# A two-layer transformer kernel on one core: weight loads swapped at the start, larger pieces at the end, and a new written-out order for TensorE

## The chip, the cores and the metric

The kernel runs on one NeuronCore of a Trainium2 chip. The metric is the device time of one execution, in microseconds. Besides the runs there is one profiled execution, from which all traces come. TensorE (PE) does the matmuls, and its weight loads (PEld) overlap them; VectorE (DVE) and ScalarE (ACT) move results out of PSUM and do softmax, LayerNorm and activation arithmetic; GpSimd (POOL) clears a buffer and does one small power; SyncE (SP) issues nearly all DMAs. Every engine works through its instructions in order.

## The reference

Two layers over `x` of 2048 rows by 576 columns (bf16). Each layer is attention with a recurrent memory and then a gated FFN, with the same weights in both layers:

```python
for s in range(n_seg):                       # 64 segments of 32 rows
    h = concat([mem, layernorm(x)[s]])       # 8 memory rows + 32 rows
    q, k, v = h @ Wq, h @ Wk, h @ Wv         # 32 heads of 128
    p = softmax(where(mask, q @ k.T * scale, -1e9))
    o = (p @ v) @ Wo
    mem, out[s] = o[:8], o[8:]               # the next segment reads mem
x = x + out
x = x + (silu(layernorm(x) @ w1) * (layernorm(x) @ w3)) @ w2   # 4608 wide
```

A segment needs the memory of the segment before it, so attention is a chain of 64 steps in each layer.

## The kernel before

**Steps.** The second layer runs eight segments behind the first (`LAG = 8`), so there are 72 steps. In most of them a segment of layer 0 and one of layer 1 are handled together (80 columns instead of 40); the first eight steps have layer 0 alone and the last eight layer 1 alone. After every four steps (128 rows) an FFN "job" follows for each layer that has the rows, cut into 18 pairs of 128-column blocks ("pr"), whose work is spread over the next steps. The last job has one layer only, and nothing to be spread over.

**Letters.** All TensorE work is cut into batches, one letter each. In a step: `Q` and `q` are the Q and K projections of four heads (units u0 to u7; `Q` the four 128-row chunks of the weights, `q` the last 64 rows, which need the last memory piece); `S` scores of eight heads (groups g 0 to 3); `T` transposes of the probabilities; `P` probabilities times V; `O` and `o` the output projection; `X`, `x`, `V`, `v` and `G`, `g` the V projection (VX, VM and, for pairs of steps, VG). For the FFN: `F` and `f` the up projections of a pair of blocks, `W` and `w` the down projection of two pairs (first and second layer). `p`, `n`, `a`, `b` and `m` are transposes around LayerNorm and residual. Between `S` and `T` stands the softmax chain: add of the mask, maximum and subtraction, exponential (ACT), sum and reciprocal, product into `PB`. Each letter writes PSUM banks (eight in all), and an eviction on ACT or DVE frees them.

**Order.** PE's order is written out by hand as a string: `ORDER = FIRST + FOUR * 11 + LAST`. FIRST covers the start to a steady state; FOUR is a pass of four steps (224 letters) and is repeated eleven times; LAST is the rest. A planner (`plan`) lays the nodes out in time with a modelled duration for each; PE follows the string, and for the other engines it takes what can start first, then by a priority. Nodes of kind "AD" go to ACT or DVE, whichever the plan has free sooner. So a change of a modelled duration moves evictions between the two engines, and a change of priorities moves DMAs on SP's queue. The emitted instructions are chained in the plan's order on each engine. The modelled duration of an eviction of 512 columns is `ew(512)`, which is 0.49 us on ACT and 0.60 on DVE.

**Weights.** `W` holds Wq and Wk (nine chunks of 4096 columns), `WV` holds Wv, `WO` holds Wo; they stay in SBUF. `load_qk(half)` loads half the heads (ten DMAs, 4.5 MB), `load_v` all of Wv (six DMAs, 4.5 MB), `load_o(g)` a quarter of Wo. The first three are ordered by their priorities. FFN weights do not fit beside them and are loaded pair by pair for each job into two buffers (`W13`, `W2C`). For the last job alone they are loaded into `W` and `WV`, once the last step has read what it needs there: `tail_load` does it in eight pieces of 512 columns, each with four DMAs into `W` (w1 and w3) and one into `WV` (w2), behind the last step's `Q`, `q` and V letters (`qk_done`, `v_done`) and, from the fifth piece, behind an `O` as well. Pair 16 and 17 of that job are kept from the job before. The first `Q` of u0 and of u4 in step 0 carries twelve extra matmuls of 512 columns on the arriving weights, if it comes ahead of its `q`.

Of the kernel before, what the change touches and what calls it, by code (L numbers as in the profile page):

```python
# [13 lines left out]
P = 128  # L14
R64 = 64
D = 576
# [10 lines left out]
NG = 4  # L27
# [153 lines left out]
def ew(*ns):  # L181
    return (actc(*ns), dve(*ns))


def ewh(*ns):
# [2 lines left out]


FIRST = (  # L190
    "maQqqqQQSQqqqQTQSqqQSQSXxvVPTPTOPOTOoooPOoQQQqqVSqqvQQqqSQQqqSQTXPSxTOPTPOTOPoooOoaQQqqqqQSvQVSqQQqTQSqqQSPTPOOT"
    "ooPTPOOooQQqqqvqSVQQQqSTQqqQPSqQOSoTXPTOPTOPxooOoQQpQqqqqQSVSnvqQFffqFQQTSqqPQOToSfFPWTOPfFTOPFOfoooWQQfqqqQSvVF"
    "qfQFQWSqqQFSfQTQPqqfFOTSoWPFTOPfxXTFPOOoooWQQqqfqQQSfqFSvVfqqQFQWSqTQQPFqffTOSoPWOTFPFTOPfaOoooWQFQqqfQSVvqqfFQQ"
    "SqWQQqqqQSTPSTbOPoXTOPTxxPOOoooXqqQpQQqqSVvnQFFSfqQqfqQQTSqfFPQTOPSofWTOPFOTFPWOoooFQqqffQQqSQQQqqgqGTSWPQQfqqFF"
    "fgSSTGGPFgfTOWPOfgGTOPFOooooWQQfqqqFQvSfqFQQfqSVTFQqfFQPSaTWQPfqqFOSoTWFOPffFTOPWOoooFQqqqfQQSWQqqQQSqqTbQSGgqgQ"
    "PGTGPSggOTGPOTOPoooOoQQppqqVqqvSQQnnQFSfqfqFTQQPFSqqfQTwOPWFSoffTOFPwTOPWOoooFQffqqFQwWSQQFfqqfFTGqqgSQPQFWTQSgf"
    "qqGQwPFTSfggOGGPOTwPOOooooWFfqqQQFQqfqvVSQQWFfqqSQwTFPaSqfqQTQwFWPSffTOPFOOTwPWOooooFqqfqQQWqSQQQSqqqQQbQSqggGTG"
    "PGTSggPGTOPOTwPOOoooo"
)
FOUR = (  # L200
    "QqQpQpQqqqvVSSnnQFffqqFQQTFSffqqQPFTWSPOwTFPOTOPwOooooWQQqqqfQSQQQqqqfFGgfSSTFPFQqfqgGQTWwPFTSfggGFPGOTOPOOooooW"
    "wQQqqqfQFQvfqfVSSwFQWQFqffqFWTQPwTFSffqqQOPWoSwTFPFOTOPwWOoooffFQqqQWQSqqqQaQSbQQTQqqqgGSSgPGTGPOTggGPOTwPOOoooo"
)
LAST = (
    "QQpqqqQpSqqQQnVqvSnQTQQPqqSFTSffOPFOTFPfwTOPFOooooWQQqfqqQFwWSfqfQQFGSgfqqQTFPGwSTWFqfgqQQPWTFSfgfgGFwGPOTOPOOoo"
    "oofFWQwQFqfqqQQWSfqVvSQFTFqqfQPQTwSqqfFOQPWwffSFTFPOOTFPWOoooowQQqqqfQQSvqqqVSQWTQQPqqQOTSSbPwvVoXTOPToxPOOooVpp"
    "qqvQQQqqSQQnnQqqfSFQTFPSfqqQTFfSPOOwTWPFfTOPFOoooowQWfqqQQQFvqqfVSSFQQfqqFTWQfqqSQPwTOPoSXfTFPOWOTxfPFOwoooFQQvq"
    "fqVSqqQQWwFTQqfqfSQQPFwFqfqSQTWOPSfFTFWPOTOPwOooooffQFqqQWQSqqqQwFvSfVQTQPWqqQSOQqwTSbPOTXoPToxPOOooQqqqqQpQQSVv"
    "QnqSQFqfqfFQTQqSPSwTOPFFTffoPOTOPwOoooFQqqfqQQqfvSVFQFQSqfqQTQQqfqSFPSXTwPOTFPOTxooPOOoowQQqqvfSVqqqQQQSqQQTSfFP"
    "FTfqqQOoSPwTfOFPFTOPfooOowQQqqqqQSQQSqfqFQVvSfFTwQQqfqPTSFPFTOPOTOPwOooooffpFnwFfffFFFwffFFwfffFFwFwfffFFFwfffFF"  # L210
    "wFwFffffFFww"
)
ORDER = FIRST + FOUR * 11 + LAST

# [1 line left out]
class Opt:  # L216

    qk, qkt, sc, tr, pv, wo, wog, vm = 0.0079, -0.0342, 0.0268, 0.1447, 0.0406, 0.2653, 0.0725, 0.1407
# [4 lines left out]
def make_nodes(em, nseg, pools, o=Opt, dma_bw=230e3, load_bw=400e3):  # L223
# [4 lines left out]
    def node(*a, **k):  # L228
        n = Node(*a, **k)
        nodes.append(n)  # L230
        return n
# [5 lines left out]
    kb = lambda rows, cols: rows * cols * 2  # L237
# [9 lines left out]
    def load(name, nbytes, prio, fn, deps=()):  # L247
        return node("DMA", nbytes / load_bw, fn, deps=deps, prio=prio, name=name, lat=2.0)

    ld_m0 = node("ACT", 0.1, em.load_m0(), prio=-90, name="m0", lat=2.5)  # L250
    ld_h = [load("ldqk", kb(512 + 2 * R64, 4096), half - 9.0, em.load_qk(half)) for half in (0, 1)]
    ld_v = [load("ldv", kb(512 + 2 * R64, 4096), -7.0, em.load_v())]
    ld_o = [load("ldo", kb(1024, 576), g - 6.0, em.load_o(g)) for g in range(NG)]

    b = banks(1)
    m0t = node("PE", 0.3, em.m0_tr(b[0]), deps=[ld_m0], prio=-5, mode="full", acq=b, name="m0tr")
# [42 lines left out]
    def v_nodes(name, t, k, prio, tail_at, emit, strips, deps, tail_deps, free):  # L299

        modes = ("col", "quad") if strips[0][3] == R64 else ("c32", "oct")
        b = banks()
        m_ = node("PE", 8 * 0.2158, emit(b, False), deps=deps, prio=prio, mode=modes[0], acq=b, name=name)
        n = node("PE", 0.2158, emit(b, True), deps=deps + tail_deps, prio=prio + tail_at, mode=modes[1], acq=b, name=name + "t")
        reads_ht.setdefault(t, []).extend([m_, n])
        for r in (0, 1):
            outs = em.v_parts(strips, r)
            b[r].users = len(outs)
            for p0, width, row, blk in outs:
                e = node("AD", ew(512), em.v_ev(b[r], p0, width, row, blk), deps=[m_, n] + free.get(blk // 2, []), prio=prio + 0.01 * (blk // 2),  # L310
                         rel=[b[r]], name=name + "e")
                vx_ev.setdefault((name, t, blk // 2), []).append(e)
        return [m_, n]
# [15 lines left out]

    def vg_out(t, g, b, deps, row):  # L330

        return [node("AD", ew(512), em.v_ev(b[r], row, R64, row, 2 * g + r), deps=deps, prio=t + o.vm + 0.01 * g + (0.05 if row == 0 else 0.0), rel=[b[r]],
                     name="VGe") for r in (0, 1)]

    def vx_pair(t, prio):
# [8 lines left out]
    def step(t):  # L344
        ls = layers_of(t)
        nl = 2 if both(t) else 1
        c80 = 40 * nl
        e = role(t)
# [12 lines left out]
        wos, wots = [], []  # L361
        for g in range(NG):
            qs, qe = [], []
            for u in (2 * g, 2 * g + 1):
                q = Slot("qkt", users=1)
                b = banks()
                pq = t + o.qk + o.ustep * u
                m_ = node("PE", 32 * mm80, em.qk(t, u, b), deps=hx + hm[:1] + ([ld_h[u // 4]] if t == 0 else []),
                          prio=pq, mode="full", acq=[q] + b, name="QK")
                n = node("PE", 4 * mm80, em.qk_tail(t, u, b), deps=hx + hm + ([ld_h[u // 4]] if t == 0 else []), prio=pq + o.qkt, mode="row",  # L370
                         acq=[q] + b, name="QKt")
                rd += [m_, n]
                me[f"QK{u}"], me[f"QKt{u}"] = m_, n
                for r in (0, 1):
                    qe.append(node("AD", ew(256, 64) if nl == 2 else ew(160), em.qk_ev(t, u, r, q, b[r]), deps=[m_, n], prio=t + o.ustep * u,
                                   rel=[b[r]], name="QKe"))
                qs.append(q)
            s = banks(1)[0]
            sme = Slot("sme")
            pf = t + o.gstep * g  # L380
            sc = node("PE", 8 * 0.0165 * nl, em.scores(t, g, qs, s), deps=qe, prio=pf + o.sc, mode="col", acq=[s, sme], rel=qs, name="SC")
            a = node("DVE", dve(320), em.sm_add(t, g, s, sme), deps=[sc], prio=pf, rel=[s], name="add")
            m_ = node("DVE", dve(320, 320) + 0.13, em.sm_max(t, g, sme), deps=[a], prio=pf, name="maxsub")
            c = node("ACT", 0.105 + 320 * 0.000833, em.sm_exp(t, g, sme), deps=[m_], prio=pf, name="exp")
            pb = Slot("pb")
            d = node("DVE", dve(320) + 0.2, em.sm_sum(t, g, sme), deps=[c], prio=pf, name="sum")
# [7 lines left out]
            if paired(t):  # L394
# [3 lines left out]
            b = banks()  # L398
            ot = Slot("ot")
            pv = node("PE", 8 * mm80, em.pv(t, g, pts, b), deps=pe_ + vx_ev["VM", t, g] + vx_ev["VX", t - e, g],  # L400
                      prio=pf + o.pv, mode="full", acq=b + [ot], rel=[pts], name="PV")
            pvs[t, g] = pv
            if paired(t):
# [3 lines left out]
                      acq=[y] if g == 0 else [], name="WO")  # L407
# [6 lines left out]
            wots.append(wot)  # L414
            me[f"SC{g}"], me[f"TR{g}"], me[f"PV{g}"], me[f"WO{g}"] = sc, tr, pv, wo
        if t == nst - 1:
            last_reads[2].extend(wos)
            last_reads[1].extend(me[f"{k}{u}"] for u in range(8) for k in ("QK", "QKt"))
        nxt = [li for li in ls if t - LAG * li + 1 < nseg]
        ye = []  # L420
# [17 lines left out]
        return node("DVE", dve(576), em.post_add(li, g, xr[g], b[0]), deps=[d], prio=prio, rel=b, name="POSTa")  # L438

    last_up = []  # L440
    last_reads = [], [], []
    kept = {}

    def job(j):
# [6 lines left out]
        s0 = 4 * j + 4 if j < ngrp else 4 * j - 4 + LAG  # L451
# [9 lines left out]
        w2_last = {}  # L461
        tail = None
        if last:
            v_done, qk_done, wo_done = last_reads
            tail = []
            for i in range(8):
                late = wo_done[i - 4:i - 3] if i >= 4 else []
                parts = [(0, 9 * 512, qk_done[2 * i:2 * i + 2] + late), (1, 4 * 576, v_done + late)]
                tail.append([load("tail", kb(128, c), s0 + o.tail_at + 0.01 * i, em.tail_load(i, what), deps=dep) for what, c, dep in parts])

        npp = NPR // 2
        for at, pp in enumerate([npp - 1] + list(range(npp - 1)) if last else range(npp)):
            mids, w2s, htts, lds = [], [], [], []
            stays = last and pp == npp - 1
            for pr_ in (2 * pp, 2 * pp + 1):
                prio = s0 + o.ff + (o.win if s0 + 4 < nst else o.last_win) * (2 * at + pr_ % 2) / NPR
# [7 lines left out]
                else:  # L484
# [6 lines left out]
                b = banks()  # L491
# [3 lines left out]
                          acq=b + [htt], rel=rel13, name="FF")  # L495
# [7 lines left out]
            for (bi, g) in ents:  # L503
                b = banks()
# [54 lines left out]
class Emitter:  # L559
# [126 lines left out]
    def tail_load(self, i, what):  # L686

        def f(n):
            T = self.T
            fa = i * 512  # L690
            t13, t2 = T.W[:, :, fa:fa + 512], T.WV[:, i * 4 * D:(i + 1) * 4 * D].rearrange("p (b d) -> p b d", b=4)
            if what != 1:
                for kind, wd in ((0, self.a.w1), (1, self.a.w3)):
                    self.dma(t13[:, 4 * kind:4 * kind + 4], wd[0:4 * P, fa:fa + 512].rearrange("(c p) f -> p c f", p=P))
                for kind, wd in ((0, self.a.w1), (1, self.a.w3)):
                    self.dma(t13[kind * R64:(kind + 1) * R64, 8], wd[4 * P:D, fa:fa + 512])
            if what != 0:
                self.dma(t2, self.a.w2[fa:fa + 512, :].rearrange("(b p) d -> p b d", p=P))
            for h in range(2):
                self.tail_w[2 * i + h] = (t13[:, :, h * 2 * P:(h + 1) * 2 * P], t2[:, 2 * h:2 * h + 2])  # L700
        return f


# [598 lines left out]
```

## Time and profile before

| | |
|---|---|
| five runs: median, lowest, highest | 2703.98, 2696.57, 2706.35 us |
| profiled execution: own time, span | 2704.19, 2702.4 us |
| mean granted TensorE clock | 0.992 |
| busy: PE, DVE, ACT, POOL | 2630.9, 2090.3, 1367.1, 333.6 us |
| DMA: bytes, mean rate | 321.42 MB, 119 GB/s |
| DMAs on the SP queue | 1616 |

The own time is that of the profiled execution by the clock of the runs; the span is the time between its first and last recorded instruction. Busy time is the sum of an engine's instructions without the time it waits, and a busy PE can still be slower than it might be, since matmul ends are modelled. A line of the timeline gives the start, the time, the engine, the source line, the operation, output and inputs, and in brackets the idle time ahead of it with what ended it. Since one helper emits each engine's instructions, the source line says little, and tile names are what to go by: `QKT` is q and k, `SME` and `STAT` the softmax, `PTS` the transposed probabilities, `OT` the attention output, `HTT` the FFN's middle, `XR` the residual rows.

### The profile page before, as it was taken

How to read it: one execution, taken by the hardware profiler on the slowest of the kernel's cores; microseconds unless marked ns; L12 is line 12 of the kernel's file. 1: busy time of each engine (PE TensorE's matmuls, PEld its weight loads, DVE VectorE, ACT ScalarE, POOL GpSimd, SP SyncE). 2: the span in 40 equal slices, each digit the busy share in tenths (PEclk: the TensorE clock that was granted, in tenths of full speed). 3: DMA queues.
4: the chain of work that ended last, by engine and by line, in shares of the span. 5: the costliest groups of instructions: out<-in, count | busy, mean ns of one | idle time of the engine just before them, and what ended most of it. 6: DMA issues, size and time to landing. Idle time of an engine off the chain costs nothing.

```text
span 2702.4 us, 126553 instructions
## 1 busy us (share of the span) xinstructions
PE 2630.9 (97%) x55714; PEld 2227.8 (82%) x55795; DVE 2090.3 (77%) x5376; ACT 1367.1 (51%) x4025; POOL 333.6 (12%) x400
## 2 busy tenths in 40 slices
PE   5999999999999999999999999999999999999998
PEld 3788888888888888888888888888888888888886
DVE  4787887887778778777877877787787777787876
ACT  2655554544546454554545445464545546454553
POOL 1111110110101011010101101010110101011110
PEclk8999999999999999999999999999999999999999
DMA  9064523234342433434243343424234342434358
GB/s 316 4 182 122 160 83 117 85 110 125 99 130 84 118 88 110 125 100 130 82 119 88 110 125 99 130 83 119 88 110 125 99 130 66 133 89 147 114 169 245
DMA packets 483225, 321.42 MB, mean 119 GB/s; under 512 B 26376, under 2 KB 477328, under 8 KB 482160
## 3 DMA queue, kind: packets, MB, share of 16 engines
q1 hardware_dynamic: 479488, 306.22, 38.4%
q8 instruction: 437, 7.16, 1.1%
q0 software_dynamic: 3024, 6.93, 0.9%
q14 instruction: 116, 0.95, 0.1%
q10 hardware_dynamic: 160, 0.16, 0.0%
HBM read 308.49 MB, written 2.36 MB: 115 GB/s over the span
## 4 chain that ended last, share of the span: by engine, by line
PE 87%; ACT 4%; DMA 4%; DVE 3%; issue 1%; SPq 0%; POOL 0%; DVEq 0%; ACTq 0%; POOLq 0%
PE bank L578 87%; ACT V L581 3%; DMA W<-in_B_w_dram 2%; DVE SME L584 1%; DMA W<-in_A_Wk_dram 1%; DMA WV<-in_A_Wv_dram 1%; DVE STAT L584 1%; DVE V L584 1%; ACT SME L581 0%; ACT XTB L581 0%; SPq L587 0%; ACT QKT L581 0%; ACT PTS L581 0%; DVE HTT L584 0%; DMA XN<-in_A_x_dram 0%
## 5 line engine op out<-in xcount | busy, mean ns | idle before, releaser
L578 PEld LDWEIGHTS <-W 128*128 128x128 bf16 (+1 forms) x29520 | 1238.6, 98 | 148.9 <-issue 44.0
L578 PE MATMUL bank<-HT,W 128*128 128x80 bf16 (+3 forms) x23040 | 810.2, 196 | 23.0 <-DMA W<-in_A_Wq_dram 10.7
L578 PE MATMUL bank<-XTB,W 128*128 128x256 bf16 (+3 forms) x6480 | 662.7, 261 | 7.4 <-DMA W<-in_B_w_dram 4.4
L581 ACT ACTIVATE QKT<-bank 128x256 bf16<-128x256 f32 (+3 forms) x1587 | 366.0, 316 | 369.4 <-PE bank L578 350.2
L981 POOL MEMSET PB<- 128x1024 bf16 x288 | 274.2, 952 | 1818.6 <-PE bank L578 1316.7
L578 PE MATMUL bank<-OT,WO 128*128 128x80 bf16 (+3 forms) x11520 | 406.8, 198 | 0.7 <-DVE OT L584 0.3
L581 ACT ACTIVATE V<-bank 64x512 bf16<-64x512 f32 (+1 forms) x616 | 346.4, 584 | 110.0 <-PE bank L578 104.9
L578 PEld LDWEIGHTS <-WO 128*128 128x128 bf16 (+1 forms) x11520 | 379.5, 102 | 15.6 <-issue 5.2
L578 PE MATMUL bank<-WV,HT 128*32 128x512 bf16 (+5 forms) x3160 | 358.5, 387 | 14.6 <-issue 9.9
L578 PE MATMUL bank<-W2C,HTT 128*128 128x288 bf16 x2240 | 315.3, 286 | 0.0
L584 DVE TENSOR_TENSOR PB<-SME,STAT 40x128 bf16<-40x128 f32 (+4 forms) x912 | 275.3, 336 | 14.9
L584 DVE TENSOR_REDUCE STAT<-SME 104x8 f32<-104x320 f32 (+1 forms) x576 | 273.9, 475 | 14.3 <-ACT SME L581 8.9
L581 ACT ACTIVATE HTT<-bank 128x512 bf16<-128x512 f32 (+1 forms) x324 | 179.6, 555 | 183.3 <-PE bank L578 181.3
L578 PEld LDWEIGHTS <-HT 128*32 128x32 bf16 (+4 forms) x3240 | 137.5, 97 | 159.0 <-issue 41.5
L584 DVE SCALAR_TENSOR_TENSOR XR<-bank,XR 128x288 f32<-128x288 f32 x576 | 246.5, 450 | 15.7 <-PE bank L578 7.8
L578 PEld LDWEIGHTS <-HTT 128*128 128x128 bf16 x2304 | 209.8, 98 | 48.4 <-issue 0.2
L581 ACT ACTIVATE OT<-bank 128x320 bf16<-128x320 f32 (+1 forms) x398 | 149.3, 405 | 166.7 <-PE bank L578 165.6
L584 DVE CAST QKT<-bank 128x192 bf16<-128x192 f32 (+2 forms) x461 | 125.0, 317 | 136.3 <-PE bank L578 135.1
L584 DVE SCALAR_TENSOR_TENSOR HTT<-HTT,bank 128x512 bf16<-128x512 bf16 (+1 forms) x324 | 202.5, 625 | 34.3 <-ACT HTT L581 30.4
L581 ACT ACTIVATE PTS<-bank 128x320 bf16<-128x320 f32 (+1 forms) x385 | 144.4, 402 | 164.3 <-PE bank L578 127.3
L584 DVE TENSOR_TENSOR HTT<-HTT,bank 128x512 bf16<-128x512 bf16 (+1 forms) x324 | 203.7, 629 | 30.6 <-DVE HTT L584 0.5
L581 ACT ACTIVATE SME<-SME 104x320 f32<-104x320 f32 (+1 forms) x288 | 135.5, 470 | 139.1 <-DVE SME L584 136.6
(61 smaller groups left out, 1805.5 us busy)
## 6 DMA issues: line engine op xcount, KB each, us to landing
W<-in_B_w_dram SPq DMA_DIRECT2D x612, 256.0 KB, 3.5
W2C<-in_B_w_dram SPq DMA_DIRECT2D x306, 288.0 KB, 3.2
W<-in_B_w_dram SPq DMA_DIRECT2D x612, 32.0 KB, 3.2
W<-in_B_w_dram SPq DMA_DIRECT2D x16, 512.0 KB, 8.5
WO<-in_A_Wo_dram SPq DMA_DIRECT2D x4, 1152.0 KB, 16.8
XR<-in_A_x_dram POOLq DMA_DIRECT2D x16, 288.0 KB, 2.8
WV<-in_B_w_dram SPq DMA_DIRECT2D x8, 576.0 KB, 7.2
W<-in_A_Wq_dram SPq DMA_DIRECT2D x8, 512.0 KB, 9.0
```

What stands on the lines that cost most here:

```text
L578: self.ch("PE", self.nc.tensor.matmul(out, lhsT=lhsT, rhs=rhs, start=start, stop=stop, skip_group_check=True, **k))
L581: self.ch("ACT", self.nc.scalar.activation(*a, **k))
L584: self.ch("DVE", getattr(self.nc.vector, fn_)(*a, **k))
L981: return lambda n: self.ch("POOL", self.nc.gpsimd.memset(self.T.PB[:, pb.i], 0.0))
```

## The change

The three strings are replaced; each keeps its length and its count of every letter. Three priorities put `load_v` between the two halves of `load_qk`. The eviction of a V block is modelled with 0.55 us on ACT and 0.60 on DVE, and `S` of a single-layer step with 0.23 us rather than 0.13. The last job's weights come in four pieces of 1024 columns, 20 DMAs in place of 40, without the condition on `O`. In the built program 173 instructions move from ACT to DVE over the whole kernel (5366 to 5539 on DVE); in one pass of FOUR, DVE has 20 rather than 14 evictions of QK, 13 rather than 12 of PTS, 11 rather than 10 of OT, 3 rather than 2 of VM and 10 rather than 11 of VG.

```diff
-    "maQqqqQQSQqqqQTQSqqQSQSXxvVPTPTOPOTOoooPOoQQQqqVSqqvQQqqSQQqqSQTXPSxTOPTPOTOPoooOoaQQqqqqQSvQVSqQQqTQSqqQSPTPOOT"
+    "maqQQQQqqqxvXSSVTPTPQqqQQqqSQSOoTOPToPOOooQQQqqqqQSVvSqqQTQQPQqqTSSXPOOToPTOPooxOoQQqqqqQSvQVSqQqQQQqSTqSPTPOOTo"
...
 FOUR = (
-    "QqQpQpQqqqvVSSnnQFffqqFQQTFSffqqQPFTWSPOwTFPOTOPwOooooWQQqqqfQSQQQqqqfFGgfSSTFPFQqfqgGQTWwPFTSfggGFPGOTOPOOooooW"
-    "wQQqqqfQFQvfqfVSSwFQWQFqffqFWTQPwTFSffqqQOPWoSwTFPFOTOPwWOoooffFQqqQWQSqqqQaQSbQQTQqqqgGSSgPGTGPOTggGPOTwPOOoooo"
+    "QqQpQpQqqqVnvSSnQFfqfqFQQTFSqffqQPFTOoSwPWTOPFTOPWOooowQfqqqQQSqqqQQQFSSgffGTFPQFqqfgQGwTWPFSffggGFTGOPOTwPOOooo"
+    "oWQQQqqqqQWSSVvffqFFQTwQPFfqfqFTwWQFSfqfFQPWwSFTOOPWTOPwOooooffFQQqqqWQQSqqqQQSabQqqgQTGgSSPGTggGPGTOPOTwPOOoooo"
 )
...
-    "FTfqqQOoSPwTfOFPFTOPfooOowQQqqqqQSQQSqfqFQVvSfFTwQQqfqPTSFPFTOPOTOPwOooooffpFnwFfffFFFwffFFwfffFFwFwfffFFFwfffFF"
-    "wFwFffffFFww"
...
+    "qqSQPwSTOPfFOTfooPwTFPOOooFfqqQQQvSqqVQwSQTFqqqfQQPSqfFTQPOoSwTFPOFTOPffoOoopwnffffFFFFwFwfffFFFwfffFFFwFwfffFFF"
+    "wffFFwfffFFww"
...
-    ld_h = [load("ldqk", kb(512 + 2 * R64, 4096), half - 9.0, em.load_qk(half)) for half in (0, 1)]
-    ld_v = [load("ldv", kb(512 + 2 * R64, 4096), -7.0, em.load_v())]
-    ld_o = [load("ldo", kb(1024, 576), g - 6.0, em.load_o(g)) for g in range(NG)]
+    ld_h = [load("ldqk", kb(512 + 2 * R64, 4096), 3 * half - 9.0, em.load_qk(half)) for half in (0, 1)]
+    ld_v = [load("ldv", kb(512 + 2 * R64, 4096), -8.0, em.load_v())]
+    ld_o = [load("ldo", kb(1024, 576), g - 5.0, em.load_o(g)) for g in range(NG)]
...
-                e = node("AD", ew(512), em.v_ev(b[r], p0, width, row, blk), deps=[m_, n] + free.get(blk // 2, []), prio=prio + 0.01 * (blk // 2),
+                e = node("AD", (0.55, 0.6), em.v_ev(b[r], p0, width, row, blk), deps=[m_, n] + free.get(blk // 2, []), prio=prio + 0.01 * (blk // 2),
...
-            sc = node("PE", 8 * 0.0165 * nl, em.scores(t, g, qs, s), deps=qe, prio=pf + o.sc, mode="col", acq=[s, sme], rel=qs, name="SC")
+            sc = node("PE", 8 * (0.0165 * nl if nl == 2 else 0.029), em.scores(t, g, qs, s), deps=qe, prio=pf + o.sc, mode="col", acq=[s, sme], rel=qs, name="SC")
...
-            v_done, qk_done, wo_done = last_reads
+            v_done, qk_done = last_reads
             tail = []
-            for i in range(8):
-                late = wo_done[i - 4:i - 3] if i >= 4 else []
-                parts = [(0, 9 * 512, qk_done[2 * i:2 * i + 2] + late), (1, 4 * 576, v_done + late)]
-                tail.append([load("tail", kb(128, c), s0 + o.tail_at + 0.01 * i, em.tail_load(i, what), deps=dep) for what, c, dep in parts])
+            for i in range(4):
+                parts = [(0, 9 * 1024, qk_done[4 * i:4 * i + 4]), (1, 8 * 576, v_done)]
+                tail += [[load("tail", kb(128, c), s0 + o.tail_at + 0.01 * i, em.tail_load(i, what), deps=dep) for what, c, dep in parts]] * 2
...
-            fa = i * 512
-            t13, t2 = T.W[:, :, fa:fa + 512], T.WV[:, i * 4 * D:(i + 1) * 4 * D].rearrange("p (b d) -> p b d", b=4)
+            fa = i * 1024
+            t13, t2 = T.W[:, :, fa:fa + 1024], T.WV[:, i * 8 * D:(i + 1) * 8 * D].rearrange("p (b d) -> p b d", b=8)
```

On SP's queue the new order at the end is: W of the first piece, W2C of two pairs, W13 of pairs 16 and 17, WV of the first piece, W2C of pairs 16 and 17, WV of the second piece, W of the second, WV and W of the third, WV and W of the fourth. Before, it was W and then WV for each piece from the third on, behind the same W2C.

## The prediction

> **What bounds the kernel now.** The page comes first: the engine table and the chain say that TensorE is the path.
>
> ```profile
> PE 2630.9 (97%) x55714; PEld 2227.8 (82%) x55795; DVE 2090.3 (77%) x5376; ACT 1367.1 (51%) x4025; POOL 333.6 (12%) x400
> PE 87%; ACT 4%; DMA 4%; DVE 3%; issue 1%; SPq 0%; POOL 0%; DVEq 0%; ACTq 0%; POOLq 0%
> ```
>
> TensorE idles 71 us in all. The table by stage says where (columns: stretch, length, busy time of PE, PEld, DVE, ACT, POOL, clock, DMA share, GB/s).
>
> ```profile
> 0.00:528.66 528.66, 489.93 (x11766) 411.19 (x11778) 397.71 (x1070) 267.85 (x797) 75.55 (x97) 0.97 0.45 136
> 528.66:2262.17 1733.51, 1718.29 (x34324) 1458.76 (x34387) 1359.51 (x3454) 886.62 (x2607) 204.22 (x243) 1.00 0.37 108
> 2262.17:2620.00 357.83, 354.04 (x8250) 299.63 (x8249) 283.01 (x722) 186.21 (x545) 46.99 (x54) 1.00 0.41 119
> 2660.00:2690.00 30.00, 27.26 (x395) 22.63 (x392) 20.38 (x51) 6.86 (x17) 1.14 (x2) 1.00 1.08 335
> ```
>
> The second line is the eleven passes of FOUR: 1733.5 us, 157.48 us for nearly every pass, with only 1.4 us of PE idle in each. The rest of the idle time is at the start (weights arriving), in the first steps, and at the end (last FFN weights arriving, DMA share 1.08). The timeline of PE with its weight loads shows the two kinds of wait inside a pass and the wait at the end:
>
> ```profile
> 1172.47 0.30 PE L578 MATMUL bank<-HT,W 64*128 64x80 bf16 x7 [0.19 <-ACT V L581]
> 1305.39 0.59 ACT L581 ACTIVATE V<-bank 64x512 bf16<-64x512 f32 x1
> 1306.04 0.18 PEld L578 LDWEIGHTS <-V 128*128 128x128 bf16 x4 [0.21 <-ACT V L581]
> 2686.87 0.84 PE L578 MATMUL bank<-XTB,W 128*128 128x128 bf16 x12 [1.12 <-DMA W<-in_B_w_dram]
> 2692.08 1.05 PEld L578 LDWEIGHTS <-W 64*128 64x128 bf16 x14 [2.34 <-DMA W<-in_B_w_dram]
> ```
>
> In the first and third, PE waits for an eviction of V on ScalarE (0.59 us each, queued behind one another). In the last two it waits for the last FFN weights.
>
> **The change, part by part.** A letter of the order is one batch of matmuls; I time it from its first weight load to the next letter's, since all 55,795 weight loads are in the trace (so O with 80 columns is 1.15 us, F with 256 is 1.65).
>
> *Start.* The loads that step 0 needs keep their bytes: half of Wq and Wk, the other half, Wv (4.5 MB each) and Wo. Wo stays last, and its last quarter decides:
>
> ```profile
> L587 SPq DMA_DIRECT2D WO<-in_A_Wo_dram x4: 389/4600/8194, 32.0 to 47.5; - x4
> DMA to landing us min/median/max: 11.9/16.8/20.5
> ```
>
> Issued at 47.5 and landed 11.9 later, it is there at 59.4; O of group 3 ran at 59.7, and step 1 began at 61.2. After the change Wv lands near 33, where the second half landed before, and that half near 47.6, where Wv did. From there remain the second half's Q and q (four Q of about 1.0 us, some q and scores: 5.5), the softmax of group 3 (3.4 us from its add at 20.24 to its PB at 23.59 in step 0), T, P and two evictions (2.2): 58.7, still before 59.4. So nothing is gained, since Wo covers it, and nothing lost while the chain stays under 11.8 us. On SP's queue, Wo and the first FFN weights alone stand behind the swapped loads, with the same bytes ahead of them; on PE, all of step 0's second half now stands behind q of u4 and its wait for 47.6, with DVE and ACT idle meanwhile, where before PV and Wo's matmuls stood behind Wv's wait. The twelve 512-column warm-up matmuls move from u0 to u4, because q of u0 now comes first; both places are waits for weights. I take +0.5, from 0 to +2.
>
> *The order, by sums.* The counts of each letter are equal, so only mode changes and waits differ. FOUR has 65 mode changes before and after. By the letter that stands ahead of the change: Q −3, q +3; F +3, f −3; O +1, T −1; W −1, w +1 cancel, as the two of each pair cost the same (0.13, 0.22, 0.13, 0.24 us); G −1 (0.31) and n +1 (0.15) leave −0.16 us per pass. Over FIRST and LAST the same sums give about +0.5 and −0.1.
>
> *The order, by waits.* In a pass of before I find 1.6 us of real waits against the letters' usual times: 0.37 at the step boundary (memory eviction), 0.40 behind VM's evictions (first line of the timeline above), 0.46 and 0.20 at two P behind VG's evictions (third line), 0.18 at a VG tail. For the new order I add up the letters between producer and consumer and set that against the latency before:
> - The step boundary has the same letters: 0.
> - VM to the q that wants its banks: 4.46 us of letters before, 4.22 after; the need was 5.1 with seven evictions on ACT and one on DVE. Two go to DVE now, so it falls by one 0.58 to 4.5. The shortage goes from 0.65 to 0.3: −0.2.
> - The two P: 1.99 and 1.87 us after the VG (need up to 2.57) become 2.3 and 3.25: −0.4.
> - A VG tail now comes 0.26 us after scores whose bank it needs; the add that frees it took 0.61: +0.2.
> - Softmax to T: shortest distance 5.63 before, without a wait; now two of 5.5. One w has 2.55 us after its FFN activation, where 2.66 had no wait: +0.1 together.
> With the mode changes this makes −0.5 us per pass, −5.5 over eleven. Bounds: no more than the 1.6 can go (−18), and each new tight place could cost its whole shortage at median latency (6.13 for the softmax, 2.91 for the activation: 0.6+0.6+0.4 less the 0.6 gained, +1.0, so +11). The pass also moves eight more evictions to DVE, net: six of QK (0.63), two of 0.49 and some V, +4.8 us on 123.7 of 157.5, under 82%, so DVE is covered by PE.
>
> FIRST's single-layer steps have the same shortages by this count (5.6 and 5.3 us); in LAST's, the LayerNorm before b gets tighter (+1.1). I take +0.5 and +1, each ±4.
>
> *The last FFN weights.* Twenty DMAs fewer, equal bytes. Before, the last loads held back by PE (W13 of a kept pair, issued 2649.83) open a stream without gaps that ends with W of piece 7 at 2692.1. Afterwards the F that frees that slot stands 2.6 us earlier before the final POST. But W2 of the last piece now precedes W (its condition is met earlier), which puts 0.59 MB at 0.335 MB/us, +1.8 us, ahead of the last W. Rows of 2048 B replace 1024 B: the start moved 4096 B at 359 GB/s, the tail 335, so 7 MB take between 0 and 1.5 us less; I take 0.7, as 2048 lies between. Last W: 2692.1−2.6+1.8−0.7 = 2690.6. What then remains grows: pairs 12 to 15 rather than 14 and 15, so F12, F13 (0.85+0.89), two tails and a mode change (0.4) and w5 (1.1): +3.3. Net +1.8, from +0.5 to +4.
>
> "DMA: Bandwidth & Descriptors" of the Trainium skill (Specifications) asks for at least 512 B for line rate, which makes 1024 and 2048 B equal and speaks against the larger pieces. By it the rate term would be 0 and the tail +2.5; no run yet shows 2048 B.
>
> *Sum.* +0.5 +0.5 −5.5 +1.0 +1.8 = −1.7 on the profiled execution's 2704.2 (span 2702.4): 2702.5, and as that execution is 0.2 above the median, 2702.
>
> **Rivals.** *A, the forecast:* waits change places, −0.2 to −0.8 per pass, 2697 to 2708. *B, the search finds most of the waits:* −1.5 per pass, with the other terms 2704−16.5+3.8 = 2691.5. For it: the planner's V eviction costs rise to 0.55 and 0.60, nearer to the measured 0.58 and 0.69, and V's evictions are what PE waits for. Against it: the boundary wait of 0.37 stands in both. *C, the short places bind (slower):* DVE, 4.8 us fuller, delivers softmax later than 5.5 us, so T waits in every pass. It decides from a latency over 5.5 (median before 6.13, shortest 4.6); at +0.8 per pass, 2704+8.8+3.8 = 2716.5. Against it: T at 5.63 did not wait before, since the planner serves tight chains first. *D, the tail alone:* the larger last piece finds PE cooled down, while passes stay equal. F14 and F15 took 1.58 and 1.71 us after the wait at 2692, against 0.89; two more F like this make the tail +4 and all +6, 2710.
>
> **How the numbers follow.** A 0.45, B 0.27, C 0.23, D 0.05. A run can tell about 0.2% (5.4 us) from no change: the bounds are 2698.6 and 2709.4. Of A, 0.36 lies between them and 0.06 below; B is below, C and D above. Faster 0.33, same 0.36, slower 0.31. The range reaches from inside B to inside C: 2689 to 2715; A's own is 2697 to 2708.
>
> **What would show it.** Step 1's first QK at 61 to 63, with WO landed last. A pass of 157.0: V waits shorter, a short one at a VG tail behind an add. If passes are 156 or less, B; if T's weight loads wait for PB, C. In the tail, W as the last load, landing near 2690.6 less whatever came earlier, and 9 us of PE after it. I am wrong if a pass changes by over 1 us, or if the tail gets shorter.

## The result, and the profile after

The changed kernel takes 2706.64 us (median of 23 runs, 2703.52 to 2710.72) where the kernel before takes 2701.12 beside it (43 runs): ratio 1.002, 95% interval 1.0014 to 1.0025. It is 5.5 us slower; 1.7 us less was forecast. Its profiled execution took 2705.63 us of its own time, with a span of 2703.9.

The page of the changed kernel, its engine table and its chain:

```profile
PE 2627.6 (97%) x55722; PEld 2224.0 (82%) x55795; DVE 2137.9 (79%) x5549; ACT 1343.4 (50%) x3852; POOL 333.3 (12%) x400
PE 89%; DVE 6%; DMA 2%; issue 1%; ACT 1%; SPq 1%; POOL 0%; DVEq 0%; ACTq 0%
```

TensorE is still the path. VectorE carries 48 us more, as the moved evictions say, and stands for 6% of the chain instead of 3%. The table by stage, for the eleven passes of FOUR and for the first 486 letters of LAST (columns as before: stretch, length, busy PE, PEld, DVE, ACT, POOL, clock, DMA share, GB/s):

```profile
534.01:2267.49 1733.48, 1721.08 (x34335) 1458.01 (x34386) 1400.81 (x3608) 866.51 (x2453) 203.46 (x241) 1.00 0.37 107
2267.49:2579.10 311.61, 309.47 (x6956) 262.75 (x6956) 248.84 (x633) 158.15 (x459) 41.27 (x48) 1.00 0.40 117
```

The passes take 1733.48 us, against 1733.51 before. So the forecast gain of 5.5 is not there, and no loss either. Before, the same 486 letters took 313.74 us. What is late is late from the start. Timeline of PE in step 0 of the changed kernel:

```profile
32.20 0.62 PE L576 MATMUL bank<-WV,HT 64*32 64x512 bf16 x4 [9.46 <-DMA WV<-in_A_Wv_dram]
45.88 0.45 PE L576 MATMUL bank<-ident,PB 104*128 104x40 bf16 x8 [5.64 <-DVE PB L582]
47.62 0.43 PE L576 MATMUL bank<-PTS,V 128*128 128x40 bf16 x8 [0.32 <-ACT PTS L579]
47.87 0.59 PE L576 MATMUL bank<-W,ident 128*128 128x512 bf16 x1
48.69 3.87 PE L576 MATMUL bank<-W,ident 128*128 128x512 bf16 x10 [0.22 <-issue]
52.39 3.26 PE L576 MATMUL bank<-HT,W 128*128 128x40 bf16 x128
61.87 0.43 PE L576 MATMUL bank<-ident,PB 104*128 104x40 bf16 x8 [1.11 <-DVE PB L582]
67.15 3.96 PE L576 MATMUL bank<-HT,W 128*128 128x40 bf16 x160 [0.32 <-ACT HT L579]
```

Wv landed near 33 and the second half of Wq and Wk near 47.5, both as forecast. Two things were not. T of group 0 (second line) waits 5.64 us for its softmax, which stands behind V's evictions on DVE (four of them from 37.84 to 40.62, the softmax's first addition at 40.65). Then the warm-up matmuls (lines 4 and 5) run from 47.87 to 52.39, when the weights they were to wait for are already there: the last of the chunks that they read landed at 45.2. Step 1 (last line) begins at 67.15. In the kernel before the warm-ups ran early, while PE waited for weights, and step 1 began at 61.20:

```profile
11.29 4.05 PE L578 MATMUL bank<-W,ident 128*128 128x512 bf16 x9
15.52 1.26 PE L578 MATMUL bank<-W,ident 128*128 128x512 bf16 x3 [0.18 <-DMA W<-in_A_Wk_dram]
61.20 1.56 PE L578 MATMUL bank<-HT,W 128*128 128x40 bf16 x56 [0.32 <-ACT HT L581]
```

### The profile page after: what moved, and what is told of

It is laid out like the page before. It is cut to its first block, busy times and chain, and to the rows that moved or that the text cites. A ratio compares the mean times of both kernels' runs of the same rounds, so it can differ in the third digit from the quotient of the medians.

```text
span 2703.9 us, 126468 instructions
## 1 busy us (share of the span) xinstructions
PE 2627.6 (97%) x55722; PEld 2224.0 (82%) x55795; DVE 2137.9 (79%) x5549; ACT 1343.4 (50%) x3852; POOL 333.3 (12%) x400
## 4 chain that ended last, share of the span: by engine, by line
PE 89%; DVE 6%; DMA 2%; issue 1%; ACT 1%; SPq 1%; POOL 0%; DVEq 0%; ACTq 0%
PE bank L576 89%; DVE STAT L582 1%; DVE V L582 1%; DVE SME L582 1%; SPq L585 1%; DMA W<-in_B_w_dram 1%; DVE PB L582 1%; DMA WV<-in_A_Wv_dram 1%; ACT V L579 1%; DVE PTS L582 0%; DVE OT L582 0%; DMA W<-in_A_Wk_dram 0%; DVE LNS L582 0%; ACT QKT L579 0%; DVE XN L582 0%
## 5 line engine op out<-in xcount | busy, mean ns | idle before, releaser
L579 ACT ACTIVATE QKT<-bank 128x64 bf16<-128x64 f32 (+4 forms) x1458 | 347.1, 311 | 399.3 <-PE bank L576 364.0
L576 PE MATMUL bank<-WV,HT 128*32 128x512 bf16 (+4 forms) x3169 | 355.9, 385 | 16.8 <-DMA WV<-in_A_Wv_dram 9.9
L582 DVE CAST QKT<-bank 128x192 bf16<-128x192 f32 (+2 forms) x590 | 161.0, 318 | 108.7 <-PE bank L576 106.8
L582 DVE CAST V<-bank 64x512 bf16<-64x512 f32 (+1 forms) x256 | 175.4, 685 | 32.3 <-PE bank L576 26.6
```

Source lines behind the costliest of these rows:

```text
L576: self.ch("PE", self.nc.tensor.matmul(out, lhsT=lhsT, rhs=rhs, start=start, stop=stop, skip_group_check=True, **k))
L579: self.ch("ACT", self.nc.scalar.activation(*a, **k))
L582: self.ch("DVE", getattr(self.nc.vector, fn_)(*a, **k))
```

## The experiments

Stretches below are times from one letter's first weight load to another's, at places where both strings have the same letters behind them. The experiments call the kernel after "the changed kernel"; each ratio, with its 95% interval, is to the kernel before in the same call (medians 2704.41, 2703.94, 2703.79 and 2704.07 us) and is not the quotient of the two medians. Identical code differs between profiles by 1 to 3 us in some stretches, so a stretch is read over several profiles.

**The warm-up matmuls: taken away, then moved.**

```diff
-            for c in range(4 if first and t == 0 and u % 4 == 0 else 0):
+            for c in range(0):
```

> The changed kernel without the twelve 512-column warm-up matmuls of u4 in step 0 (their result is never read). Theory W: in the changed order they start at 47.9 us, after the weights they were to wait for have landed (45.2), and sit on the path for 4.5 us. So step 1, which began at 67.15, begins near 63.5 (a cooler TensorE gives 0.5 to 1 back), and the whole is 3.5 to 4.5 us under the changed kernel: ratio to the kernel before 1.0002 to 1.0010. Rival V: step 0 is late because the softmax of groups 0 and 1 waits on VectorE behind evictions of V (T at 45.88 after 5.64 us idle) and because the second half comes last; then PE waits elsewhere, step 1 begins at 66.5 or later, ratio 1.0018 to 1.0022.

The second kernel does the same twelve in `qk_tail` of u0, ahead of its matmuls, while PE waits for weights:

```diff
+            for c in range(4 if first and t == 0 and u == 0 else 0):
+                for _ in range(3):
+                    self.mm(self.bk(b[1])[:], self.T.ident[:, 0:P], self.T.W[:, 4 + c, u * 512:(u + 1) * 512], True, True)
```

> The changed kernel with the same twelve matmuls moved from u4 to u0, ahead of its q, where PE waits for the first weights as it did in the kernel before. Theory W: 3.5 to 5 us under the changed kernel, ratio 0.9998 to 1.0008; the first Q letters run at the full clock but PE then waits for Wv near 32 all the same, so it equals the version without warm-ups within 1 us. Rival V: as the changed kernel, ratio 1.0018 to 1.0022.

Measured: 2708.71 us, 1.0016 (1.0008 to 1.0025) without them; 2708.97, 1.0019 (1.0011 to 1.0028) with them at u0. By the times alone theory W misses both its ranges, and the second run falls into rival V's. The start says otherwise: letters 0 to 45 took 64.4 in the changed kernel, 60.75 and 59.81 here. So 3.6 to 4.6 us of the start are the warm-ups at u4. The total does not follow, since in the same two profiles the passes and the two stretches behind letter 3755 were 1 to 2 us longer each. In the first of them the Q matmuls of u4 start at once, more slowly:

```profile
46.74 4.24 PE L576 MATMUL bank<-HT,W 128*128 128x40 bf16 x128
```

**The start exchanged, whole string.** Load order and FIRST of before in the changed kernel, and the reverse.

```diff
-    ld_h = [load("ldqk", kb(512 + 2 * R64, 4096), 3 * half - 9.0, em.load_qk(half)) for half in (0, 1)]
-    ld_v = [load("ldv", kb(512 + 2 * R64, 4096), -8.0, em.load_v())]
-    ld_o = [load("ldo", kb(1024, 576), g - 5.0, em.load_o(g)) for g in range(NG)]
+    ld_h = [load("ldqk", kb(512 + 2 * R64, 4096), half - 9.0, em.load_qk(half)) for half in (0, 1)]
+    ld_v = [load("ldv", kb(512 + 2 * R64, 4096), -7.0, em.load_v())]
+    ld_o = [load("ldo", kb(1024, 576), g - 6.0, em.load_o(g)) for g in range(NG)]
...
```

> The changed kernel with the FIRST string and the load order of the kernel before; FOUR, LAST, the four pieces and the modelled costs stay changed. Theory W and rival V both say that the start holds the whole loss: step 1 at 61.2, 5 to 5.5 us under the changed kernel, ratio 0.9994 to 1.0005. Rival L: the loss of 5.5 in the medians sits in LAST and the tail (the two profiles differ by 1.5 only, and LAST moves by some us in both directions): ratio 1.0010 or more.

> The kernel before with the changed FIRST string and load order alone. Theory W and rival V: step 1 near 67, ratio 1.0016 to 1.0024, the whole of the measured loss. Rival L: 1.0010 or less.

Measured: 2715.18, 1.0039 (1.0027 to 1.0051) and 2715.93, 1.0046 (1.0034 to 1.0058). Both are worse than either kernel, and neither isolates the start: the string and the modelled costs belong together, and more than 200 evictions landed on another engine in each. In the first of them letter 45 begins at 64.5 as before, but the letters 45 to 805 lose 9.7 us; in the second they lose 6.3. Each of the two strings lost with the other's modelled costs.

**Both again, and step 0 alone.** The changed kernel and the one without warm-ups were run again. Then only the first 41 letters and the load order were exchanged, which changes 8 and 6 evictions.

> The changed kernel unaltered, so that the next three are compared with it on the same chip. Theory W and rival V: ratio 1.0015 to 1.0025, step 1 between 66.5 and 67.5 us.

> The changed kernel without the warm-up matmuls of u4, once more beside the changed kernel. Theory W (the matmuls are on the path, 3.8 us of step 0 in the first look): 2 to 4.5 us under the changed kernel. Rival I (the time won at the start is lost again, because the position of the instructions moves and PE's waits that nothing visible ends, 8.0 us in the last 140 us against 1.7 in the changed kernel, come of that): within 1.5 us of the changed kernel, and the profile shows more than 5 us of such waits in its last 140 us again.

```diff
-    "maqQQQQqqqxvXSSVTPTPQqqQQqqSQSOoTOPToPOOooQQQqqqqQSVvSqqQTQQPQqqTSSXPOOToPTOPooxOoQQqqqqQSvQVSqQqQQQqSTqSPTPOOTo"
+    "maqQqqQQSQqqqQTQSqqQSQSXxvVPTPTOPOTOoooPOoQQQqqqqQSVvSqqQTQQPQqqTSSXPOOToPTOPooxOoQQqqqqQSvQVSqQqQQQqSTqSPTPOOTo"
```

> The changed kernel with the load order and the first 41 letters (step 0) of the kernel before; all else as changed, and only 8 evictions change engine. Theory W: step 1 at 61 to 61.5, the whole 4.5 to 5.5 us under the changed kernel, ratio 0.9996 to 1.0006. Rival L (the loss is in LAST and the tail): within 2 us of the changed kernel. Rival I: the start is won, and part of it lost again in the tail, ratio 1.0006 to 1.0015.

> The kernel before with the changed load order and the changed first 41 letters alone; 6 evictions change engine. Theory W: step 1 near 67, the whole 5 us over the kernel before, ratio 1.0016 to 1.0022. Rival L: 1.0010 or less.

Measured: 1.0017 (1.0008 to 1.0027) for the changed kernel, 1.0009 (0.9999 to 1.0018) without warm-ups, 1.0011 (1.0001 to 1.002) with the old step 0, and 1.0015 (1.0006 to 1.0024) for the kernel before with the new step 0. The last is the clearest: the new step 0 alone costs 4 us (1.6 to 6.5), about three quarters of the result. Letters 0 to 45 took 58.09 with the old step and 64.12 with the new. The old step in the changed kernel missed its range: the start was won, but the ratio fell by 0.0006 only, where theory W had 4.5 to 5.5 us. It lies in rival I's range, and rival I is neither shown nor excluded: PE's waits that nothing visible ends were 5.2 us of the last 146 without warm-ups, and 4.6 in the changed kernel beside it.

**The end: pieces, string, order of the loads.** Eight pieces in the changed kernel and four in the kernel before (the diff's lines on `tail` and `tail_load`, backwards and forwards); the whole string LAST of the changed kernel in the kernel before; and in the changed kernel W ahead of W2 in each piece:

```diff
-                parts = [(0, 9 * 1024, qk_done[4 * i:4 * i + 4]), (1, 8 * 576, v_done)]
+                parts = [(0, 9 * 1024, qk_done[4 * i:4 * i + 4]), (1, 8 * 576, v_done + qk_done[4 * i + 2:4 * i + 4])]
```

> The changed kernel with the last FFN weights in eight pieces of 512 columns again (and their condition on O); no eviction changes engine, all strings are those of the change. Theory P (the prediction's tail term: a larger last piece leaves 3.3 us more of PE work behind its landing, the larger rows give 0.7 back): the last wait for W ends near 2691 as in the changed kernel, but only about 9 - 3.3 = 6 us of FFN work stand behind it, so 2.6 us less than the changed kernel's own runs (2706.6 to 2710.3): ratio to the kernel before about 1.0008 to 1.001. If W of the last piece also comes ahead of its W2 again, another 1.8 less: 1.0002. Theory N (the pieces do not matter: the end is set by the last byte of the stream, and the FFN work behind it is caught up while waiting): the ratio stays at 1.0017 to 1.002. From step 71's first letters (start of letter 3769) to the last letter: 112 to 116 us in all runs of the changed kernel; P makes it 109.5 to 113, N leaves it.

> The kernel before with the last FFN weights in four pieces of 1024 columns and nothing else changed: strings, modelled costs and load order at the start are those of before, no eviction changes engine. Theory P: +3.3 for the work behind the last piece, +1.8 if W2 of the last piece goes ahead of its W, -0.7 for the rows: +2.6 to +4.4 us, ratio 1.001 to 1.0016, and the post-step stretch after the last wait for W grows from 10 to 13 us. Theory N: 1.000 within 0.0008, with the waits for W redistributed (fewer and longer). If larger rows raise the rate of the last 7 MB clearly above 335 GB/s, the last W lands before 2691 and the ratio falls below 1.

> The kernel before with the string LAST of the changed kernel alone: FIRST, FOUR, load order, modelled costs and the eight pieces are those of before. 36 evictions of LAST are on another engine than in the changed kernel. Theory L (the gain of 2.0 us that every run of the changed kernel shows in the first 200 letters of LAST belongs to that string): 143.8 falls to 141.8 us there, and if the FFN letters that stand earlier before the end (2.6 us by the prediction) start the last stream earlier as well, another 1 to 2.6 us at the end: ratio 0.9983 to 0.9993, faster than both kernels. Rival M (the gain comes from the state in which the new FOUR leaves the evictions at its end, not from LAST): 143.8 stays, and the ratio is 1.000 to 1.001.

> The changed kernel with one condition more: the W2 of each of the four last pieces also waits for the last K letters that its W waits for, so that W goes ahead of W2 on the SP queue, in each piece. No eviction changes engine. Theory P (the prediction's +1.8 for 0.59 MB ahead of the last W): the last wait for W ends 1.8 us earlier and the time falls by up to 1.8: ratio 1.001 to 1.0014 where the changed kernel has 1.0017 to 1.002. Rival: W2 is needed soon after as well, and the stream starts later since W2 can no longer use the time before the K letters: 0 to +1 us, ratio 1.0018 to 1.0025.

Measured: 2706.01, 1.0006 (0.9998 to 1.0014) with eight pieces; 2707.49, 1.0017 (1.0008 to 1.0026) for before with four; 2704.31, 1.0008 (0.9999 to 1.0016) for before with the new LAST; 2711.6, 1.0025 (1.0014 to 1.0036) with W first. Four pieces are a loss in both kernels (theory P). From letter 3855 to the last letter:

| | eight pieces | four pieces |
|---|---|---|
| LAST of before | 68.5, 68.6 | 70.7 |
| LAST of the changed kernel | 63.1, 63.2, 62.3, 62.6 | 65.5 to 70.1, mean 68.3 (7 profiles) |

The new string gains 5.8 us here, and the four pieces give 5.5 of it back. PE's waits over the last 146 us show a part of how, first in the second profile of the changed kernel:

```profile
PE bank L576 <- issue: 4.6, 5, 3.1
PE bank L576 <- DMA W<-in_B_w_dram: 4.1, 2, 3.7
```

and with eight pieces:

```profile
PE bank L578 <- issue: 4.0, 3, 2.7
PE bank L578 <- DVE YTS L584: 0.9, 1, 0.9
```

The wait for W (total, times, longest) is gone in this profile; in the other three with the new LAST and eight pieces it is 1.4 to 1.9 us, and in the seven with four pieces nothing to 5.8. The other part is the clock granted to PE. In five of the seven, those whose last wait for W was 2.2 us or longer, it falls to 0.5 about the end of that wait and stays there for 3.4 or 6.8 us; behind last waits of 1.4 us or less, with four pieces or eight, it does not. The same 5 us in the changed kernel and in the fastest version below (the last three columns are the clock, the DMA share and GB/s):

```profile
2687.00:2692.00 5.00, 1.40 (x12) 1.03 (x13) 0.73 (x2) 0.00 (x0) 0.00 (x0) 0.83 0.29 75
2687.00:2692.00 5.00, 4.44 (x56) 3.50 (x56) 2.81 (x8) 0.77 (x2) 0.00 (x0) 1.00 0.09 29
```

From letter 3855 to the last, PE idles for 8.6 us on average in the seven profiles with four pieces and works at half clock for 6.7; in the four with eight pieces it is 5.8 and 0.9. The idle time makes 2.8 us of the 5.5, and the clock, at half of the time worked under it, an estimated 2.9.

W first was no gain: the last wait for W ended 111.7 us after letter 3755, against 111.5 and 113.1 in the two profiles of the changed kernel, since the stream also began 1.8 later than in the first of them, as the rival said. The new LAST in the kernel before gains in the tail, and its first 200 letters take 141.76 us as in the changed kernel, where the kernel before takes 143.78: that gain is the string's, as theory L said. But its first 486 letters took 314.33 instead of 311.61. There some forty evictions stand on another engine than in the changed kernel. PE's waits in 2268 to 2640 begin with

```profile
PE bank L578 <- DVE PB L584: 3.5, 4, 1.3
```

a line that the changed kernel does not have there. So that run does not say what the string alone is worth in all.

**What was left open, and a version against both.** The old step 0 with eight pieces; then the new load order with no warm-ups and the scores ahead of V, with four pieces and with eight. The second's edit beside the warm-ups:

```diff
-    "maqQQQQqqqxvXSSVTPTPQqqQQqqSQSOoTOPToPOOooQQQqqqqQSVvSqqQTQQPQqqTSSXPOOToPTOPooxOoQQqqqqQSvQVSqQqQQQqSTqSPTPOOTo"
+    "maqQQQQqqqSSxvXVTPTPQqqQQqqSQSOoTOPToPOOooQQQqqqqQSVvSqqQTQQPQqqTSSXPOOToPTOPooxOoQQqqqqQSvQVSqQqQQQqSTqSPTPOOTo"
```

> The changed kernel with the load order and first 41 letters of before (as in the run with the old step 0) and with eight pieces of 512 columns at the end (as in the run with eight pieces): of the change, FOUR, LAST, the rest of FIRST and the modelled costs remain. Theory S (the loss lies in the start and in the pieces, and nowhere else): step 0 takes 58 to 59.1 us again, the first 200 letters of LAST keep 141.76, the stretch from letter 3769 to the end is 107 to 111 us as with eight pieces: together 2.0 to 4 us better than before, ratio 0.9986 to 0.9994. Rival R (the old step 0 still measured 1.0011, so some 3 us are lost in the new FIRST behind step 0 or in the passes): the two gains are eaten, ratio 0.9998 to 1.0008, and letters 45 to 3269, which are 2197.7 us in the profile of before, take 2200 or more.

> The changed kernel without the 24 warm-up matmuls of its first step (as in the run without them), and with the two score letters of groups 0 and 1 moved ahead of x, v, X in step 0, so that their softmax comes ahead of V's evictions on DVE; 9 evictions of step 0 change engine. Theory V (softmax behind V's evictions delays the step): T of group 0 starts at 39 to 41 us rather than at 44.3 to 44.7, the T, P pairs are over by 42 to 43, and Q of u4 starts with the landing of the second half near 46.3 to 46.7; the end of the step moves by up to 1.5 us, letters 0 to 45 from 60.5 to 59. Rival O (Wo's last quarter, landing near 60, and the second half's landing set the end whatever stands ahead): T moves but letters 0 to 45 stay at 60.0 to 60.7. In ratio 1.0 us is 0.0004: between 1.0005 and 1.0015, which the times alone will not tell; the stretches do.

> The same (no warm-ups, early scores), with eight pieces of 512 columns at the end: the best start that Wv between the halves gives here, with the better end. Theory S: start +0 to +1.5 against before, first 200 letters of LAST -2.0, stretch from letter 3769 -2 to -5: ratio 0.9985 to 1.0, within 0.0005 of the run with the old step 0 and eight pieces, which would say that the load order itself costs next to nothing once the warm-ups and the place of the scores are right. Rival R (3 us are lost in letters 45 to 3269): 1.0 to 1.001. If the load order itself costs, this run is 2 us or more behind the one with the old step 0 and eight pieces.

Measured: 2702.99, 0.9997 (0.9986 to 1.0008); 2708.72, 1.0015 (1.0005 to 1.0024); 2705.53, 1.0005 (0.9995 to 1.0016). The first is the fastest version and no slower than the kernel before; that it beats it is not shown. Taking both named losses away takes the result away. Theory S had forecast a gain, and 0.9997 lies just outside its range. The letters 45 to 3269 took 2200.9 us, as rival R has it; but four profiles with the code of before have 2197.7 to 2201.9 there, so rival R is not shown either. (The warm-ups left out are twelve, as the first experiment says: the weight loads fall from 55795 to 55783.) The timeline of PE in the last of the three, with the load order of the change:

```profile
39.37 0.37 PE L578 MATMUL bank<-ident,PB 104*128 104x40 bf16 x8
42.51 0.45 PE L578 MATMUL bank<-PTS,V 128*128 128x40 bf16 x8 [0.39 <-ACT PTS L581]
47.40 3.07 PE L578 MATMUL bank<-HT,W 64*128 64x40 bf16 x95 [0.69 <-DMA W<-in_A_Wk_dram]
57.90 3.06 PE L578 MATMUL bank<-OT,WO 128*128 128x40 bf16 x80
61.28 2.89 PE L578 MATMUL bank<-HT,W 128*128 128x40 bf16 x82 [0.32 <-ACT HT L581]
```

T now starts at 39.4 and no longer waits, PE is back at waiting for the second half, and step 1 begins at 61.28, where it began at 61.20 before. In the run with four pieces the last of these weights came 2.3 later and letters 0 to 45 took 60.55 (59.25 here), against 58.6 with the old order. So 0.7 to 2 us remain with the new load order. Both kernels lack warm-ups, though, and the kernel before has them at u0, where they were worth 0.8 us above (59.81 against 60.6); early scores with warm-ups at u0 were not run, so what the order itself costs is not isolated. T moved as theory V said; of the end of the step, one profile agrees with theory V (59.25) and one with rival O (60.55).

## Why the prediction was wrong, point by point

Where the time went, by stretches (mean and extremes over profiles that share the code of that stretch):

| letters | code of before | code of the change | difference | forecast |
|---|---|---|---|---|
| 0 to 45 | 58.6 (58.0 to 59.3; 5) | 64.1 (63.5 to 64.4; 5) | +5.5 | +0.5 |
| 45 to 805 | 464.9 (463.3 to 466.8; 4) | 466.3 (464.4 to 467.8; 11) | +1.4 | +0.5 |
| 805 to 3269, the passes | 1734.6 (1733.5 to 1735.2; 4) | 1735.3 (1733.5 to 1736.6; 11) | +0.7 | −5.5 |
| 3269 to 3755 | 313.8 (313.7 to 314.0; 3) | 311.7 (311.4 to 312.0; 11) | −2.1 | +1.0 |
| 3755 to 3855 | 52.5 (51.8 to 53.2; 3) | 52.6 (51.5 to 53.6; 11) | +0.1 | with the line above |
| 3855 to the last | 68.5 (68.5 to 68.6; 2) | 68.3 (65.5 to 70.1; 7) | −0.2 | +1.8 |

The differences add up to +5.4, and +5.5 was measured. Two steps failed.

**The start (+0.5, "from 0 to +2").** The landings were right: 33 for Wv, 47.6 for the second half, 59.4 for Wo. The chain was not: 58.7 was given, and the last T, P and O ran to 66.8. The step that failed is the sentence on the warm-up matmuls, "both places are waits for weights", which priced them at nothing. The 58.7 has no term for them. At u4 the wait was over before they could start, because PE had its own chain to finish first (the late T). They cost the 4.5 us from 47.87 to 52.39, and gave 1.0 back: the 128 QK matmuls behind them took 3.26 us, and 4.24 without them. The net 3.5 agrees with 64.1 against 60.6 for the two profiles without them. Of the remaining 2, the late softmax is 0.7 (from 60.6 to 59.9 with early scores, two profiles each, which differ among themselves by as much); the rest goes with the load order and was not isolated. With warm-ups and late softmax both gone, the last P ended at 58.1, near the forecast's 58.7. The clock granted was 0.5 from 45.0 to 51.8, and the ten warm-ups of the second line ran at 0.39 us each, against 0.24 for a 512-column matmul inside a pass (1.67 us for 7). "TensorE: Matmul & The Clock Gate" of the Trainium skill (Part 1: The HAM clock gate) says that the warm-up is about 3.4 us of time, at half speed, whatever is issued in it. The rows agree. By that rule a warm-up behind the landing can only cost.

**The passes (−5.5).** The waits that were to go did go. PE's waits over the eleven passes, before:

```profile
PE bank L578 <- issue: 7.0, 44, 0.2
PE bank L578 <- ACT HT L581: 3.8, 11, 0.3
PE bank L578 <- ACT V L581: 1.9, 10, 0.2
```

and after:

```profile
PE bank L576 <- issue: 3.8, 23, 0.3
PE bank L576 <- ACT HT L579: 3.8, 11, 0.3
PE bank L576 <- ACT QKT L579: 0.2, 1, 0.2
```

The wait for V is gone, the waits without a named cause are half, and the boundary wait (HT) stayed, as forecast. This is about the 5 us that the sum had. But a quiet pass fell only from 157.48 to 157.45. PE's idle time in the passes shrank by 2.8 us (1733.51−1718.29 to 1733.48−1721.08) and its busy time grew by 2.8. Against the shortest time of the same letter in either kernel (taken separately with and without a change of mode behind it), a pass of before loses 8.9 us and one of after 9.2. The 0.40 at VM's q fell to nearly nothing and the 0.65 at two P to 0.5, and F behind the LayerNorm write (0.34), another q (0.25), two T and a g (0.2 each) are new. The step that failed is the count of "real waits" as 1.6 us per pass: it was a list of the places that stood out, while half of the 9 us stands in some forty places of 0.05 to 0.2 that a new order shuffles. (One of its terms does not follow from its own numbers either: the shortage at VM was to fall from 0.65 to 0.3, which is 0.35, and 0.2 was booked.) Rival A's mechanism ("waits change places") was right, its net gain was none. Rival B, passes of 156 or less, did not come. Rival C is excluded by the second list, in which no T waits for PB. The reason why this new order keeps the same 9 us was not found.

**LAST (+1.0) and the tail (+1.8).** LAST's first part gained 2.1 in every profile of the change, on the other side of the forecast but inside its ±4. The tail's sum came out near, but partly by luck. The changed kernel's PE timeline at the end:

```profile
2680.20 0.84 PE L576 MATMUL bank<-XTB,W 128*128 128x128 bf16 x12 [1.62 <-DMA W<-in_B_w_dram]
2686.16 0.28 PE L576 MATMUL bank<-XTB,W 64*128 64x128 bf16 x4
2690.58 3.77 PE L576 MATMUL bank<-XTB,W 64*128 64x128 bf16 x36 [4.13 <-DMA W<-in_B_w_dram]
2695.26 2.40 PE L576 MATMUL bank<-XTB,W 64*128 64x128 bf16 x44
2697.50 2.31 PE L576 MATMUL bank<-WV,HTT 128*128 128x288 bf16 x16
```

The last W came at 2690.6, the forecast's figure, and 13.3 us of the span were left behind it where before had 10.3: +3.0, with +3.3 forecast. The first agreement is luck. The 2690.6 was to hold less whatever came earlier, and here letter 3755 came 3.2 us later than before. Counted from that letter the last W came 111.5 us behind it (113.1 in the second profile) and 116.2 before: 3.1 to 4.7 us earlier, where the sum had 1.5. Three terms were mis-sized. The W2 ahead of W was priced at 1.8, and moving it brought no gain. The earlier F letters were priced at 2.6, and the new string as a whole gained 5.8 with eight pieces. The four pieces cost 5.5 beside it (2.2 in the kernel before), against 3.3 less 0.7. What the sum left out of both is the clock, which rival D alone had: in the timeline above 36 matmuls behind the wait of 4.13 take 3.77 us, and the 44 of the next such row 2.40. Rival D was given 0.05. Its cooled-down PE is in the profiles of before as well (6.8 and 10.0 us at half clock from letter 3855 on); the new string with eight pieces is nearly rid of it, and four pieces bring it back. With eight pieces, the same end in the fastest version is

```profile
2687.55 2.51 PE L578 MATMUL bank<-XTB,W 64*128 64x128 bf16 x40 [1.45 <-DMA W<-in_B_w_dram]
2689.90 2.30 PE L578 MATMUL bank<-WV,HTT 128*128 128x288 bf16 x16
```

one short wait, and two pairs behind it instead of four. Open remain the 1.4 us of FIRST behind step 0 and the 0.7 of the passes, which are within the spread of the profiles and were not isolated.

## What to carry to other kernels

Work that fills a wait is free only where the wait is: when an order changes, ask for each filler whether its data are there before its engine is, and take it out if so. A list of the waits that stand out is not what a new order can win; compare every batch with its shortest time first, and if the loss is spread over forty places, expect the sum to stay. Larger pieces of a stream that ends the kernel leave more work behind the last one, and the longer wait ahead of it can halve the clock behind it as well (here from 2.2 us on); an order made with one set of modelled costs must be kept with them.

## What the runs showed of the hardware

The length of a DMA's rows mattered above 1 KB. With the DMA engines full, a packet of 2048 B took 94 ns of an engine in the changed kernel's tail (21.8 bytes per ns), and packets of 1024 and 1152 B took 52 and 60 ns in the tail of before (19.7 and 19.2). In the changed kernel's tail, in stretches of 5 us with the DMA engines full (last column GB/s),

```profile
2672.00:2677.00 5.00, 5.00 (x86) 4.51 (x84) 4.10 (x10) 1.54 (x4) 0.00 (x0) 1.00 1.06 371
2677.00:2682.00 5.00, 3.38 (x41) 2.63 (x40) 2.51 (x7) 0.38 (x1) 0.00 (x0) 1.00 1.07 291
2682.00:2687.00 5.00, 4.45 (x73) 3.78 (x72) 3.98 (x11) 1.54 (x4) 0.00 (x0) 1.00 1.06 385
```

In the first and last of them the W rows of 2048 B prevail, in the second the W2 rows of 1152 B. The stretches of before, with 1024 and 1152 B, lie between 334 and 346. Over 2662 to 2687 the means are 351 and 338, so 7 MB take 0.8 us less; the forecast took 0.7. "DMA: Bandwidth & Descriptors" (Specifications), which lets every row from 512 B on run at line rate, differs from this, and the measurement decides.

PE also waited with nothing released ("issue") for 1.7 to 8.0 us of the last 146 us, up to 3.1 at a time, in places that differ from profile to profile of the same code, and for 0.2 or 0.3 at most at a time in the passes of nine of the seventeen profiles, where the DMA share is 0.37 (up to 1.4 in the others). The trace shows packets of the instruction queue on the same, then full, DMA engines; that PE waits for its instructions there was not tested.
